# A Fourier mixing layer and a routed MLP on one core: earlier half-batch routing, another order of the first loads, and wider pieces of w2

## The chip, the cores and the metric

The kernel runs on one core of a Trainium2 chip. The metric is the device time of one execution in microseconds. The profile comes from one further execution, whose own span is longer.

## The reference

The input x has shape 8 x 2496 x 256. The first half is the real part of a two-dimensional Fourier transform of each batch. The 19,968 resulting rows go through eight experts, one for each row. All arithmetic is f32.

```python
X = np.fft.fft(np.fft.fft(x, axis=1), axis=2).real.reshape(B * S, D)   # S = 2496, D = 256
logits = X @ w_gate                        # 8 experts
e = argmax(logits, axis=1)
gate = softmax(logits)[row, e[row]]
y[row] = gate[row] * (relu(X[row] @ w1[e[row]]) @ w2[e[row]])   # w1: 256 x 1024, w2: 1024 x 256
```

## The kernel before, in words

Each batch passes three stages, and the rows of all batches then pass in blocks through the experts.

`first(b)` loads x in three quarters `q`. For each quarter `load_x` issues `xl`, a plain load on SP's queue, and `xh`, an indirect gather on POOL's queue that brings the mirrored rows; quarter 0 also loads `x0`. `fold` and `fold_d` add and subtract on VectorE (L290 to L284), `half1` multiplies by the table `w1` of waves (matmuls `s`), ScalarE copies the result to `t1` (L307), and `t1` is written to a DRAM scratch `Td` (L337). Each step ends in a `yield`; there are 12 steps, three for each of four values of `q`.

`regroup(b, h)` reads `Td` back in another layout into `t4` (L350); it needs all three writes. `second(b)` starts with `turn_last` (matmul `pr`), then makes ten windows of 128 rows in two halves of five (matmuls `p`, results `zz`, `rows` and the logits `lg`). After each half `route` takes the arg max, ranks the rows within each expert by matmuls `rk`, and scatters the rows into the DRAM buffer `Xs` by ten indirect stores on POOL's queue (L454). Every expert has its own region of `Xs`. `base` holds how far each region is filled.

`plan` turns `base` on VectorE into a table of blocks: first row and expert of each. `rounds()` fixes how many blocks of which size are made after which batch. Before: two of 256 rows and four of 128 after batch 0, four of 256 after batch 1, then blocks of 512, and 256s and 128s to end with; 66 blocks in all.

`experts` goes through the blocks in that order. For each block `fetch` reads row and expert from the table on SP (L509, L510) and issues three loads on SP's queue: the rows `xb` (L512), `w1` (L515) and `w2` (L517), 1 MB each for the weights, with three buffers of each. `turn` transposes the rows on TensorE; matmuls `ph` and a relu, by turns on ScalarE (L572) and VectorE (L570), give `hT`; matmuls `py` give the output, which ScalarE scales and POOL scatters. In the profile an f32 matmul of the code appears as two matmul instructions.

The order on each engine is the order in which the program issues instructions: `tc.manual_schedule()` leaves it as written. The loop at the end takes one step of `experts` at a time (a `yield 1` or `2` counts as work, `yield 0` as none) and then runs some steps of `side`, which holds the next batch's `first`, this batch's `second` and the plans. `sent` and `taken` tell the framework which scatters a fetch of rows must wait for: those up to its own round's.

At the start, before the change, seven steps of `first(1)` run ahead of `second(0)`, the rest beside it:

```python
    early = ahead_of(1)
    for _ in range(7):
        next(early)
    for k, _ in enumerate(second(0)):
        if k % 2 == 0:
            next(early, None)
```

Of the kernel before, what the change touches and what calls it, by code (L numbers as in the profile page):

```python
# [130 lines left out]
def rounds():  # L131

    want = [((256, 2), (128, 4)), ((256, 4),)] + [((512, B),)] * (B - 2)
    plan, used = [], 0

    def full(done, size):
        return max(0, -(-(done - used - E * (size - 1)) // size))

    for b in range(B):
        done = (b + 1) * S
        now = []
        for size, most in want[b]:
            k = min(full(done, size), most)
            if k:
                now.append((size, k, False))
            used += size * k
        if b == B - 1:
            k = full(done, BLK)  # L150
            used += BLK * k
            now.append((BLK, k, False))
            now.append((REST, (NT - used + E * (REST - 1)) // REST, True))
        plan.append(now)
    return plan


def in_order():

    todo = []  # L160
    for b, now in enumerate(rounds()):
        parts = [[(b, size, last, i) for i in range(k)] for size, k, last in now]
        if b == B - 1:
            few, many = parts[-2:]
            n = len(many) // len(few)
            rest = [x for i, y in enumerate(few) for x in [y] + many[n * i:n * (i + 1)]] + many[n * len(few):]
            parts = parts[:-2] + [rest]
        todo += sum(parts, [])
    return todo


TICKS = 44
WARM = 12
MOST = max(k for now in rounds() for _, k, _ in now)


# [15 lines left out]
def kernel(ctx: ExitStack, tc, x, w_gate, w1, w2, out):  # L192
# [18 lines left out]
    def put_row(dst, idx, rows, last, group):  # L211
        return unordered(pool.indirect_dma_start(  # L212
            out=dst, out_offset=bass.IndirectOffsetOnAxis(ap=idx, axis=0),
            in_=rows, in_offset=None, bounds_check=last, oob_is_err=False), group)


    def sent(ins, b):
        tc.declare_no_dep(ins, group="taken", reason="no block before this batch's round has these rows")
        tc.add_to_no_dep_group(f"xs{b}", ins)

    def taken(ins, b):
        ins = getattr(ins, "ins", ins)
        if b + 1 < B:
            tc.declare_no_dep(ins, group=f"xs{b + 1}", reason="a block has rows of its round's batches alone")
        tc.add_to_no_dep_group("taken", ins)


# [83 lines left out]
    def load(b, q):  # L311
        if b < B:
            ahead[b, q] = load_x(b, q)
        if b < B and q == 0:
            n = NP if b + 1 < B else NA
            x0 = xp.tile([NP, D], F32, tag="x0", name="x0")
            nc.sync.dma_start(out=x0[0:n], in_=xall[NA * b:NA * b + n, 0])
            ahead[b, "x0"] = x0[0:NA]

    def first(b):  # L320

        pm0 = xp.tile([NA, D], F32, tag="pm0", name="pm0")
        for q in range(NQ + 1):
            f = iter(())
            if q < NQ:
                xl, xh = ahead.pop((b, q))
                f = fold(xl, xh, q)
            next(f, None)
            yield
            if q:  # L330
                t1 = xp.tile([NP, 4, D], F32, tag="t1", name="t1")
                half1(b, q - 1, 0, pm, pm0, t1)
            next(f, None)
            yield
            if q:
                half1(b, q - 1, 1, pm, pm0, t1)
                nc.sync.dma_start(out=Td[b][:, 4 * (q - 1) * D:4 * q * D], in_=t1[:].rearrange("p j d -> p (j d)"))  # L337
                load(b + 1, q - 1)
            next(f, None)
            if q == 1:  # L340
                fold_d(pm0[:], ahead.pop((b, "x0")), 1)
            pm = xh
            yield
# [68 lines left out]
    def route(b, h, rows, lg):  # L412
# [38 lines left out]
        vec.tensor_tensor(nxt[:], rk[:, NSL], base[:], op=ALU.add)  # L451
        base = nxt
        for s in range(NSL):
            sent(put_row(Xs, pi[:, s:s + 1], rows[:, s], E * CAP - 1, "xs"), b)  # L454
            yield


# [47 lines left out]
        tabs[b, size, last] = tab  # L505

    def fetch(b, size, tab, i):
        n = size // 128
        row = nc.sync.value_load(tab[:, 0, i:i + 1], min_val=0, max_val=ROWS - size)  # L509
        ev = nc.sync.value_load(tab[:, 1, i:i + 1], min_val=0, max_val=E - 1)  # L510
        xb = bp.tile([128, BIG // 128, W], F32, tag="xb", name="xb", bufs=3)
        taken(nc.sync.dma_start(out=xb[:, 0:n].rearrange("p t c -> p (t c)"),  # L512
                                in_=Xs[ds(row, size)].rearrange("(p t) c -> p (t c)", t=n)), b)
        w1_sb = bp.tile([128, 2, F], F32, tag="w1", name="w1_sb", bufs=3)
        nc.sync.dma_start(out=w1_sb[:], in_=w1[ds(ev, 1)].rearrange("o (c p) f -> p (o c) f", p=128))  # L515
        w2_sb = bp.tile([128, FC, D], F32, tag="w2", name="w2_sb", bufs=3)
        nc.sync.dma_start(out=w2_sb[:], in_=w2[ds(ev, 1)].rearrange("o (c p) d -> p (o c) d", p=128))  # L517
        return xb, w1_sb, w2_sb

    def turn(size, xb):  # L520

# [11 lines left out]
    def experts(todo):  # L533
# [2 lines left out]

        got, xT = [], None

        def fetch_some(k, most=3):

            while k + len(got) < len(todo) and len(got) < most and todo[k + len(got)][:3] in tabs:
                b, size, last, at = todo[k + len(got)]
                got.append(fetch(b, size, tabs[b, size, last], at))

        for k, (b, size, last, at) in enumerate(todo):
            n, m = size // 128, BIG // size
            if not k:
                while todo[0][:3] not in tabs:
                    yield 0
                fetch_some(0)  # L550
                for _ in range(9):
                    yield 0
                for xT in turn(size, got[0][0]):
                    pass
# [7 lines left out]
            for f in range(FC // m):  # L562
                ph = psh.tile([128, m, size], F32, tag="h", name="ph")
                for j in range(m):
                    for c in range(2):
                        mm(ph[:, j], w1_sb[:, c, (m * f + j) * 128:(m * f + j + 1) * 128], xT[:, c, 0:size],
                           c == 0, c == 1)
                o = hT[:, m * f:m * (f + 1), 0:size]
                if f % 2:
                    vec.tensor_scalar(o, ph[:], 0.0, None, op0=ALU.max)  # L570
                else:
                    act.activation(o, ph[:], ACTF.Relu)  # L572
                yield 1
# [17 lines left out]
    def pads(b):  # L591

        ti = cp.tile([128, E], I32, name="ti")
        vec.tensor_scalar(ti[:], base[:], con["lane"][:], None, op0=ALU.add)
        for e in range(E):
            sent(put_row(Xs, ti[:, e:e + 1], pad[:], ROWS - 1, "xs"), b)
            yield

    def woven(*parts):
# [7 lines left out]

    def close(b):

        for size, k, last in rounds()[b]:  # L610
            yield from plan(b, size, k, last)

    def ahead_of(b):

# [16 lines left out]
    vec.memset(ones[:], 1.0)  # L631
    act.dma_start(out=con["w1"][:, 0:4], in_=waves[:, 0:4])
    load(0, 0)
    act.dma_start(out=con["w1"][:, 4:], in_=waves[:, 4:])
    for _ in range(WARM):
        pw = psy.tile([128, D], F32, tag="y", name="py")
        mm(pw[:], ones[:], bc(ones[:], 1, 2))
    load(0, 1)
    load(0, 2)
    act.dma_start(out=con["rt"][:], in_=const_dram("rt", consts["rt"]))  # L640
    act.dma_start(out=wg[:], in_=w_gate.rearrange("(c p) e -> p c e", p=128))
    nc.sync.dma_start(out=table[:], in_=const_dram("table", packed))
    nc.sync.dma_start(out=bt[:], in_=const_dram("blocks", cv))
    sent(unordered(nc.sync.dma_start(
        out=Xs[E * CAP:].rearrange("(k p) w -> p k w", k=BLK // 128), in_=bc(pad[:], 1, BLK // 128)), "xs"), 0)
    warm = cp.tile([1, 1], F32, name="warm")
    vec.memset(warm[:], 0.0)
    act.activation(warm[:], warm[:], ACTF.Exp)
# [2 lines left out]
    todo = in_order()  # L651
    for _ in first(0):
        pass
    regroup(0, 0)
    regroup(0, 1)
    vec.tensor_copy(tri[:], con["tri"][:])
    for c in range(2):
        pg = pm_.tile([128, E], F32, tag="m", name="pg")
# [5 lines left out]
            vec.tensor_scalar(con["rd"][:, c, to + E:to + 2 * E], pg[:], con["sgn"][:], None, op0=ALU.mult)  # L664
        else:
            vec.tensor_copy(con["rd"][:, c, to + E:to + 2 * E], pg[:])
    early = ahead_of(1)
    for _ in range(7):
        next(early)
    for k, _ in enumerate(second(0)):  # L670
        if k % 2 == 0:
            next(early, None)
    work = experts(todo)
    for b in range(1, B):

        side, done, due = mixed(b), 0, 0.0
        if b == 1:
            side = woven(close(0), chain(early, side))
        total = 16 * sum(k * size for size, k, _ in rounds()[b - 1]) / BIG
        while done < total:  # L680
            w = next(work)
            done += w
            due += TICKS * w / (0.7 * total) if w else 1
            while due >= 1:
                next(side, None)
                due -= 1
        for _ in side:
            pass
# [27 lines left out]
```

## Time and profile before

| | before |
|---|---|
| time, median of 3 runs | 1382.49 us (1381.39 to 1383.51) |
| span of the profiled execution | 1422.8 us |
| TensorE busy | 1338.3 us (94%), clock 0.970 in the mean |
| VectorE, ScalarE, GpSimd busy | 382.6, 283.8, 350.8 us |
| moved by DMA | 248.81 MB in 134,517 packets, 93,839 of them under 2 KB |

TensorE (PE) is nearly always busy, but matmuls are pipelined, so the share alone does not say how fast it works. The granted clock has to be read beside it: it is low in some slices of the first 230 us and full in the rest. SP and its queue carry plain loads and stores, ACT's queue a few loads at the start, POOL's queue every gather and scatter.

### The profile page before, as it was taken

Reading aid. Unit: us, or ns where it says so; the run is one execution under the profiler, and the core shown is the slowest. Engines: PE = TensorE matmul, PEld = TensorE weight load, DVE = VectorE, ACT = ScalarE, POOL = GpSimd, SP = SyncE. Lnnn points to the kernel's source line nnn. Section 1 sums busy time; section 2 is a strip of 40 time slices with the busy share of each in tenths; the row PEclk is TensorE's granted clock in tenths of the full one; section 3 lists DMA queues with packets and bytes.
Section 4 is the critical chain, followed back from the end, with each engine's and each line's share of the span. In section 5 each row is a group of like instructions: output and inputs, shape, how many; then the busy total and the mean of one; then the engine's idle time right before and its main releaser. Section 6 shows DMA issues by size and latency. Waiting matters only on the chain.

```text
span 1422.8 us, 17245 instructions
## 1 busy us (share of the span) xinstructions
PE 1338.3 (94%) x6186; PEld 1016.2 (71%) x6186; DVE 382.6 (27%) x1206; ACT 283.8 (20%) x656; POOL 350.8 (25%) x360
## 2 busy tenths in 40 slices
PE   4658798998999999999999999999999999999998
PEld 3557687776676667776676667776667779999997
DVE  3453243333242222322132321333211111111111
ACT  1322122132132211221122211221111111111111
POOL 1243314333314311234113311224221111111111
PEclk9768899999999999999999999999999999999999
DMA  8859777644546452561435342333442248788883
GB/s 228 204 184 291 242 240 235 246 135 117 209 131 206 135 173 90 179 187 64 168 105 166 131 175 89 108 111 107 168 143 93 89 136 269 264 265 267 268 272 102
DMA packets 134517, 248.81 MB, mean 175 GB/s; under 512 B 11245, under 2 KB 93839, under 8 KB 134432
## 3 DMA queue, kind: packets, MB, share of 16 engines
q1 hardware_dynamic: 114438, 194.38, 42.8%
q0 software_dynamic: 19344, 52.37, 10.8%
q10 hardware_dynamic: 650, 0.97, 0.3%
q8 instruction: 49, 0.80, 0.2%
q14 instruction: 36, 0.29, 0.1%
HBM read 194.28 MB, written 54.83 MB: 175 GB/s over the span
## 4 chain that ended last, share of the span: by engine, by line
PE 55%; issue 31%; POOL 5%; another core or an unknown queue 3%; DMA 2%; DVE 2%; ACT 1%; POOLq 0%; SPq 0%; DVEq 0%; ACTq 0%
PE py L197 22%; PE ph L197 22%; PE p L197 6%; POOL out_dram L212 4%; PE s L197 3%; PE pt L528 1%; DMA xh<-in_x_dram,ix 1%; POOL Xs L212 1%; DMA Td<-t 1%; DMA t<-Td 0%; DVE hT L570 0%; DVE rows L406 0%; DMA xb<-Xs 0%; POOLq L212 0%
## 5 line engine op out<-in xcount | busy, mean ns | idle before, releaser
L197 PE MATMUL ph<-xT,w_sb 128*128 128x512 f32 (+2 forms) x2112 | 589.3, 433 | 7.7 <-ACT hT L572 2.3
L197 PE MATMUL py<-w_sb,hT 128*128 128x256 f32 x2608 | 584.6, 381 | 8.5 <-DVE hT L570 8.5
L197 PEld LDWEIGHTS py<-w_sb,hT 128*128 128x128 f32 x2608 | 489.4, 191 | 72.1 <-DVE hT L570 9.3
L197 PEld LDWEIGHTS ph<-xT,w_sb 128*128 128x128 f32 x2112 | 340.2, 192 | 205.3 <-issue 176.5
L212 POOL DMA_INDIRECT out_dram<-y,ro x163 | 159.2, 977 | 861.7 <-ACT y L585 832.5
L570 DVE TENSOR_SCALAR hT<-ph 128x512 f32<-128x512 f32 x163 | 112.7, 692 | 716.6 <-issue 350.5
L585 ACT ACTIVATE y<-py,xb 128x256 f32<-128x256 f32 x163 | 77.3, 474 | 625.0 <-PE py L197 537.5
L212 POOL DMA_INDIRECT Xs<-rows,pi x160 | 159.1, 994 | 122.8 <-issue 76.1
L572 ACT ACTIVATE hT<-ph 128x512 f32<-128x512 f32 x163 | 97.3, 597 | 324.1 <-PE ph L197 287.7
L529 DVE TENSOR_SCALAR xT<-pt,table 128x512 f32<-128x512 f32 (+1 forms) x94 | 63.3, 674 | 66.7 <-PE pt L528 63.8
L197 PE MATMUL s<-xh,w 104*112 104x256 f32 (+2 forms) x208 | 62.0, 424 | 17.6 <-DVE xh L284 13.9
L197 PEld LDWEIGHTS p<-table,t 120*128 120x128 f32 x352 | 56.8, 211 | 29.2 <-issue 19.8
L197 PE MATMUL p<-table,zz 128*128 128x145 f32 (+1 forms) x320 | 60.0, 315 | 15.7 <-issue 8.0
L197 PE MATMUL p<-table,t 120*128 120x120 f32 (+1 forms) x352 | 59.6, 296 | 11.1 <-issue 4.1
L404 DVE COPY lg<-p 128x16 f32<-128x16 f32 x80 | 14.0, 175 | 203.8 <-ACT zs L401 148.0
L197 PEld LDWEIGHTS p<-table,zz 128*128 128x128 f32 x320 | 48.7, 207 | 20.0 <-issue 11.1
L197 PEld LDWEIGHTS s<-xh,w 104*112 104x112 f32 x208 | 39.8, 205 | 30.3 <-DVE xh L284 15.1
L528 PEld LDWEIGHTS pt<-table,xb 128*128 128x128 f32 x326 | 40.7, 142 | 17.7 <-issue 11.6
L528 PE MATMUL pt<-table,xb 128*128 128x128 f32 x326 | 51.6, 274 | 1.7 <-DMA xb<-Xs 1.7
L406 DVE SCALAR_TENSOR_TENSOR rows<-p,zs 128x129 f32<-128x129 f32 x160 | 48.4, 344 | 1.6 <-issue 0.6
L274 POOL DMA_INDIRECT xh<-in_x_dram,ix x24 | 24.3, 1014 | 80.4 <-PE s L197 59.8
L375 ACT COPY zz<-p 128x240 f32<-128x240 f32 (+1 forms) x88 | 31.1, 353 | 54.1 <-PE p L197 36.8
(84 smaller groups left out, 333.1 us busy)
## 6 DMA issues: line engine op xcount, KB each, us to landing
w_sb<-in_moe_w_dram SPq DMA_DIRECT2D x132, 1024.0 KB
xb<-Xs SPq DMA_DIRECT2D x28, 516.0 KB
Td<-t SPq DMA_DIRECT2D x24, 448.0 KB
xl<-in_x_dram SPq DMA_DIRECT2D x21, 448.0 KB
t<-Td SPq DMA_DIRECT2D x8, 720.0 KB
t<-Td SPq DMA_DIRECT2D x8, 600.0 KB
xb<-Xs SPq DMA_DIRECT2D x13, 258.0 KB
xb<-Xs SPq DMA_DIRECT2D x25, 129.0 KB
```

Source lines behind the costliest of these rows:

```text
L197: nc.tensor.matmul(o, lhsT=lhsT, rhs=rhs, start=start, stop=stop, **kw)
L212: return unordered(pool.indirect_dma_start(out=dst, out_offset=bass.IndirectOffsetOnAxis(ap=idx, axis=0), in_=rows, in_offset=None, bounds ...
L274: pool.indirect_dma_start(out=xh[:].rearrange("p j d -> p (j d)"), out_offset=None, in_=xrows, in_offset=bass.IndirectOffsetOnAxis(ap=ix[: ...
L375: act.copy(zz[:, :, g * GP:g * GP + n], p2[:])
L404: vec.tensor_copy(lg[:, k:k + 2], p3[:, NY:NY + 2 * E].rearrange("p (m e) -> p m e", m=2))
L406: vec.scalar_tensor_tensor(rows[:, k + m, 0:NY], p3[:, 0:NY], zs[:, 0:1], zs[:, 1:], op0=ALU.add, op1=op)
L528: nc.tensor.transpose(pt[:, c, t], xb[:, 2 * h + t, c * 128:(c + 1) * 128], ident[:])
L529: vec.tensor_scalar(xT[:, :, 256 * h:256 * h + 128 * n], pt[:].rearrange("p c t k -> p c (t k)"), con["alt"][:], None, op0=ALU.mult)
L570: vec.tensor_scalar(o, ph[:], 0.0, None, op0=ALU.max)
L572: act.activation(o, ph[:], ACTF.Relu)
L585: act.activation(y[:, i], py[:], ACTF.Copy, scale=xb[:, i, D + 1:D + 2])
```

## The change

- Blocks: after the first half of batch 0 a round of two 128-row blocks is planned and started; one 256-row block fewer follows, 67 blocks in all. Rounds are numbered from this one, so batch `b` closes round `b + 1`; `sent` and `taken` are shifted to match.
- Start: `x0` is loaded with quarter 1 and folded one quarter later. Only the first piece of the wave table stays on ACT's queue; its rest, `table`, `rt` and `wg` go to SP's queue between and behind the x of batch 0. The loads of batch 1 are no longer issued inside `first(0)`: quarters 0 and 1 come ahead of the two reads of `Td[0]` on SP, quarter 2 behind them, then the block constants and the padding rows of `Xs`. The warming matmuls go from 12 to 16.
- `Td` of batches 0 and 1 is written from ACT's queue.
- `first(1)` runs wholly inside `second(0)`, at the steps listed in `FILL`. From step 11 on the plan of the new round runs beside the first half's scatters; after step 20 the fetches of its blocks are issued, then the reads of `Td[1]`.
- `fetch` is split: for the very first block the weights are requested ahead of the rows, for others rows first as before.
- A partition of `w2` takes two neighbouring rows, so that a piece is 2 KB instead of 1 KB; to match, the stationary operand of `ph` takes every second column of `w1`.

```diff
-    want = [((256, 2), (128, 4)), ((256, 4),)] + [((512, B),)] * (B - 2)
+    want = [((128, 2),), ((256, 1), (128, 4)), ((256, 4),)] + [((512, B),)] * (B - 2)
...
-    for b in range(B):
-        done = (b + 1) * S
+    for b in range(B + 1):
+        done = b * S if b else 2 * 128 * HW - NB
...
-WARM = 12
+WARM = 16
+FILL = (0, 1, 2, 3, 4, 5, 6, 8, 9, 10, 11, 12, 13)
+
+AFTER = 5 + HW
...
-        if b + 1 < B:
-            tc.declare_no_dep(ins, group=f"xs{b + 1}", reason="a block has rows of its round's batches alone")
+        for later in range(b + 1, min(b + 3, B + 1)):
+            tc.declare_no_dep(ins, group=f"xs{later}", reason="a block has rows of its round's batches alone")
...
-        if b < B and q == 0:
+        if b < B and q == 1:
...
-                nc.sync.dma_start(out=Td[b][:, 4 * (q - 1) * D:4 * q * D], in_=t1[:].rearrange("p j d -> p (j d)"))
-                load(b + 1, q - 1)
+                (nc.sync if b > 1 else act).dma_start(out=Td[b][:, 4 * (q - 1) * D:4 * q * D], in_=t1[:].rearrange("p j d -> p (j d)"))
+                if b:
+                    load(b + 1, q - 1)
             next(f, None)
-            if q == 1:
+            if q == 2:
...
-            sent(put_row(Xs, pi[:, s:s + 1], rows[:, s], E * CAP - 1, "xs"), b)
+            sent(put_row(Xs, pi[:, s:s + 1], rows[:, s], E * CAP - 1, "xs"), b + 1 if b or h else 0)
...
-        nc.sync.dma_start(out=w2_sb[:], in_=w2[ds(ev, 1)].rearrange("o (c p) d -> p (o c) d", p=128))
-        return xb, w1_sb, w2_sb
+        return xb
+
+    def chunk(w1_sb, c, f):
+        return w1_sb[:, c, f // 2 * 256 + f % 2:(f // 2 + 1) * 256:2]
...
+        nc.sync.dma_start(out=w2_sb[:].rearrange("p (c j) d -> p c (j d)", j=2),
+                          in_=w2[ds(ev, 1)].rearrange("o (c p j) d -> p (o c) (j d)", p=128, j=2))
...
-                fetch_some(0)
-                for _ in range(9):
+                fetch_some(0, first=True)
+                for _ in range(5):
...
-                        mm(ph[:, j], w1_sb[:, c, (m * f + j) * 128:(m * f + j + 1) * 128], xT[:, c, 0:size],
-                           c == 0, c == 1)
+                        mm(ph[:, j], chunk(w1_sb, c, m * f + j), xT[:, c, 0:size], c == 0, c == 1)
...
     load(0, 0)
-    act.dma_start(out=con["w1"][:, 4:], in_=waves[:, 4:])
+    load(0, 1)
+    nc.sync.dma_start(out=con["w1"][:, 4:], in_=waves[:, 4:])
+    load(0, 2)
+    nc.sync.dma_start(out=table[:], in_=const_dram("table", packed))
+    nc.sync.dma_start(out=con["rt"][:], in_=const_dram("rt", consts["rt"]))
+    nc.sync.dma_start(out=wg[:], in_=w_gate.rearrange("(c p) e -> p c e", p=128))
...
+    load(1, 0)
+    load(1, 1)
     regroup(0, 0)
     regroup(0, 1)
+    load(1, 2)
+    nc.sync.dma_start(out=bt[:], in_=const_dram("blocks", cv))
...
-    early = ahead_of(1)
-    for _ in range(7):
-        next(early)
+    early = first(1)
+    work = experts(todo)
+    first_blocks = plan(0, *rounds()[0][0])
     for k, _ in enumerate(second(0)):
-        if k % 2 == 0:
+        if k in FILL:
             next(early, None)
-    work = experts(todo)
+        if k > AFTER:
+            next(first_blocks, None)
+        if k == AFTER + 2 * HW:
+            for _ in early:
+                pass
+            next(work)
+            regroup(1, 0)
+            regroup(1, 1)
```

## The prediction

> **What bounds the kernel now.** I read the page's slices first, then the busy times by stage, then the timeline of the first 112 us and the sync queue's own waits. The stages, with columns stretch, length, busy us (and count) of PE, PEld, DVE, ACT, POOL, then TensorE clock, DMA share and GB/s:
>
> ```profile
> 0.00:17.60 17.60, 2.74 (x12) 1.23 (x12) 3.03 (x9) 1.49 (x2) 3.54 (x8) 1.00 0.92 215
> 17.60:29.50 11.90, 11.20 (x35) 8.10 (x35) 5.74 (x17) 3.52 (x6) 2.35 (x3) 1.00 0.76 202
> 29.50:44.70 15.20, 4.33 (x12) 2.82 (x12) 8.38 (x20) 1.17 (x2) 1.67 (x2) 0.55 0.90 238
> 44.70:70.00 25.30, 20.49 (x132) 17.88 (x132) 11.91 (x59) 12.76 (x39) 7.06 (x8) 0.84 0.81 205
> 70.00:100.80 30.80, 15.43 (x57) 13.02 (x57) 17.59 (x73) 5.47 (x17) 17.86 (x16) 0.58 0.50 169
> 100.80:250.00 149.20, 129.38 (x727) 114.58 (x728) 50.02 (x189) 34.86 (x91) 48.35 (x49) 0.91 0.81 253
> 250.00:1416.00 1166.00, 1153.62 (x5210) 857.87 (x5209) 285.96 (x842) 224.02 (x499) 269.02 (x276) 1.00 0.49 164
> ```
>
> From 250 us to the last output TensorE is busy 1153.6 of 1166 us at full clock: its backlog sets the end, and only what it loses earlier can be recovered. Before 250 us it is idle for 66.4 us (250 less the six busy sums, 183.6), of which 46.6 fall before 100.8 us, when the first expert matmul runs. The timeline tells what it waits for (start, length, engine, line, operation):
>
> ```profile
> 14.99 1.22 DVE L290 TENSOR_TENSOR xl<-xl,xh 104x1020 f32<-104x1020 f32 x1 [13.69 <-DMA xh<-in_x_dram,ix]
> 29.46 0.31 SPq L337 DMA_DIRECT2D Td<-t  x1
> 38.04 0.91 SPq L350 DMA_DIRECT2D t<-Td  x2
> 44.74 0.54 PE L197 MATMUL pr<-t,table 120*120 120x6 f32 x2 [7.31 <-DMA t<-Td]
> 93.50 0.39 SPq L512 DMA_DIRECT2D xb<-Xs  x1
> 94.08 0.41 SPq L515 DMA_DIRECT2D w_sb<-in_moe_w_dram  x1
> 100.79 0.48 PE L197 MATMUL ph<-xT,w_sb 128*128 128x256 f32 x1 [1.11 <-DVE xT L529]
> 111.31 3.62 PE L197 MATMUL py<-w_sb,hT 128*128 128x256 f32 x16
> ```
>
> The serial start is visible: x at 15, the last Td write takes 29.5 to 38.0, its read back to 44.7, and then no weight is requested before 94.1. The sync queue's waits name the reason: it stood in front of the first plan and of the row scatter, with the weights queued behind.
>
> ```profile
> SPq L509 <- DVE p_n L500: 17.0, 1, 17.0
> SPq L512 <- DMA Xs<-rows,pi: 8.1, 1, 8.1
> ```
>
> [...]
>
> **The change part by part.**
>
> *Start.* ACT's queue keeps only 182 KB of w1; the rest of w1 (500 KB), rt, wg and table stand on SP behind the x that is used first, x0 behind the second quarter, pad rows and bt far later. The first xh (416 KB) landed at 15.0 while three queues shared 215 GB/s. With two in competition I put it 2 to 3 us sooner (bounds 0 to 5; a loss is excluded, since less stands beside it). Four warming matmuls add 1 us inside the idle 13.6. Fold and matmuls of batch 0 follow at their pace (29.5-17.7): last t1 at about 26.5.
>
> *Td and batch 1.* Td of batches 0 and 1 goes out from ACT; SP issues loads (1,0) and (1,1), then the two reads of Td, then (1,2). The last Td write took 8.6 us beside them. What must move by its landing: 4.2 MB of start, 1.4 MB of Td and 2.3 MB of batch 1 (two xl, three xh, x0), 7.9 MB; at 238 GB/s 33 us (bounds 31, by Td's own 8.6 less its share of neighbours, and 38, no change). The first read back (720 KB) took 6.6 with 600 KB and batch 1 beside it; I take 4, so `pr` at 37 instead of 44.7. Load (1,2), bt and the pad rows (258 KB) follow on SP, where nothing else waits until 60. Each issue costs ACT some 0.3 us, six in all, beside PE waits: nothing.
>
> *First half.* Before ran 7 steps of first(1) ahead; now all 12 lie inside second(0), so DVE folds of 2.7 us a quarter come between windows: five windows at 0.8 us DVE plus 3.9 us of folds, after 4 us from `pr` to the first window (44.7 to 52.4 less 3.8 us of s matmuls): 41 to 49. Route and the remaining folds: 3.5 + 2.4 + waits, 55. The steps of first(1) also issue the x of batch 2 now, on SP (1.5 MB, before any weights) and POOL (three gathers of 1.0 us, the last between two scatters); the DMA stage they fall in is the one before had them in. Before's first half ended at 62.5 (L451 base).
>
> *A plan more.* Its DVE work ran from 76.1 to 82.7 with a fold of 2.9 in it: 3.7 by itself, I take 4.5. It ends near 60; the value loads follow and the first w1 leaves at 61.5 instead of 94.1. The second half's windows and route stand behind the plan on DVE: they end at 69 instead of 76. That DVE delay costs PE nothing: it has no other work until rows arrive.
>
> *Blocks.* Ten scatters at 1.28 us start-to-start (63.42 to 75.01), with one xh gather between: 55.6 to 70. A block of the first round waits for this half's scatter alone: its rows can be fetched at 72, its weights lie there already, transposes at 76, `ph` at 76.5 to 80 (32 matmuls in 3.73 us). On SP, xb of block 1, its 2 MB of weights, then both reads of Td(1) are queued behind that scatter: issue 74.5; 2 MB at 350 GB/s take 6, so Td(1)'s first half is there at 82.5. In before it was issued at 63.2. PE reaches `pr` of batch 1 after block 0's `ph` (five side steps ahead of the block, two per `ph` group) and waits from 80 to 82.5; `py` and block 1 are queued behind.
>
> *Sum.* At 82.5 us PE has done one block's `ph` and transposes, 3.8 us. Before, at 100.8, had done, of the following batches, 28 `p` of 120 columns and 4 transposes at 0.11 us each, 16 `p` of 145 columns at 0.125 and 8 `s` at 0.216: 7.2 us (the pace from the chain of waits: `pt` x4 in 0.44, `py` x16, 256 columns, in 3.46). The change is at that point 3.4 us later, at 85.9: 14.9 us ahead. One block more (67 for 66) costs PE about 0.3 us, and 2.1 MB, 8 us of transfer at 253 GB/s, hidden because the first 4 MB of weights move from 94 to 110 us into 61 to 80, a stretch at 169 to 205 GB/s. The stage 100.8 to 250 loses 20 us idle and 11.6 of clock (0.09 of 129); I keep these as they are: net **14.5 us**. Made against the profiled span 1422.8, which is 40 us above the runs at 1382.5; I carry the difference over in microseconds, 1382.5 - 14.5 = **1368**.
>
> *2 KB pieces of w2.* A stretch of 4 KB pieces alone moved 350 GB/s, one of 1 KB pieces (407 of 498 packets) 386: no gain is shown. Bounds: 1.05 MB at the one rate or the other differ by 0.3 us, on some ten blocks that wait for transfers 3 us, in either direction; I take 0.
>
> *Stationary step of two.* LDWEIGHTS of a 128-column `ph` comes every 0.117 us (32 in 3.76), as often as its matmul. [...] I take nothing.
>
> **Rivals.**
>
> *The step of two slows the load.* [...] For it: PEld is busy 3.76 of 3.73 us there. [...] Chance 0.10.
>
> *The moved wait eats the gain.* Td(1)'s read now stands behind the scatter, two xb and 2 MB on SP; if instruction flow or scatter slip by 15 us, PE stands at `pr` as long as it did before. In the trace DVE stood 16.5 us at 146 with the releaser unknown, so slips of this size exist. Also the case that the two blocks don't run early because all of second(0) is ahead of them. 1376 to 1392, around 1382; chance 0.16: 0.07 within 0.2% and 0.09 above.
>
> *The late losses go too.* With weights ahead of rows and transfers begun 30 us sooner, half of the 31 us lost from 100.8 to 250 vanishes: 1368 - 16 = 1352. Against: per 128-row block 2.1 MB for 7.3 us of PE, 290 GB/s, beside the FFT's transfers. Chance 0.16.
>
> **How the numbers follow.** Forecast 0.58 (1358 to 1378 by itself), rivals 0.10, 0.16, 0.16. A measurement of this kernel can tell 0.2%, 2.8 us. Faster: 0.58 + 0.16 = 0.74; same 0.07; slower 0.09 + 0.10 = 0.19. The range from 1346 to 1390 leaves out the stride case and the tails of the others.
>
> **What would show it.** Right: first `pr` near 37 us, first w1 issue near 61 (not 94), first `ph` near 76, `pr` of batch 1 near 82 with a DMA t<-Td wait of 2 to 3 us; packets under 2 KB falling by 66 x 1024 to some 26,000; 128-column `ph` still 32 in 3.7 us. Wrong: LDWEIGHTS of `ph` above 3.8 us for 32, `pr` of batch 1 past 95, or TensorE idle before 250 us still above 60.

## The result and the profile after

The change took 1395.49 us (median of four runs, 1390.69 to 1396.66) against 1383.00 for the kernel before on the same chip (1381.39 to 1385.85). The ratio is 1.0081, with an interval from 1.0052 to 1.0111. It is slower by 0.8%, or 12.5 us; a gain of 14.5 us had been forecast.

Chips differ here, and without that several numbers below can't be understood. On some chips the kernel before takes 1383 to 1384 us, and its profile has no wait whose releaser is unknown (the profile writes "remote"). On others it takes 1410 to 1425 us, and its profiles there have 48 to 89 us of such waits, summed over the engines. I call them quiet and noisy chips; among the experiments only one chip was met at two times, and it was noisy both times, so it could also be a matter of the hour. By these marks the comparison above was on a quiet chip, and the profile of before that I predicted from, with its span of 1422.8 us, came from a noisy one.

The stages of the profile after, in the same stretches and columns as shown of before:

```profile
0.00:17.60 17.60, 4.68 (x19) 2.50 (x20) 3.05 (x9) 1.49 (x2) 3.53 (x8) 0.74 0.90 218
17.60:29.50 11.90, 10.14 (x37) 7.30 (x35) 6.75 (x19) 3.51 (x6) 2.92 (x3) 0.67 0.94 265
29.50:44.70 15.20, 5.66 (x30) 5.42 (x31) 3.23 (x9) 2.44 (x8) 0.00 (x0) 0.66 0.91 229
44.70:70.00 25.30, 16.03 (x112) 13.31 (x110) 20.53 (x97) 11.08 (x33) 11.81 (x12) 0.86 0.78 239
70.00:100.80 30.80, 14.26 (x71) 13.10 (x71) 10.81 (x42) 1.60 (x4) 13.35 (x12) 0.67 0.89 262
100.80:250.00 149.20, 137.94 (x825) 123.99 (x824) 62.51 (x238) 41.34 (x108) 58.67 (x59) 0.98 0.77 254
```

The last stage looks like a large gain: 137.94 us busy for 129.38. It is none of the change's doing, as the experiments show: on a quiet chip the kernel before is busier there still (144.57 us, in e11). The stage from 70 to 100.8, where the first block was to come early, is no better filled than before (14.26 for 15.43), although DMA now moves 262 GB/s there instead of 169. The timeline tells why (start, length, engine, line, operation, and in brackets the idle time ahead):

```profile
39.04 0.54 PE L201 MATMUL pr<-t,table 120*120 120x6 f32 x2 [10.51 <-DMA t<-Td]
61.67 0.41 SPq L516 DMA_DIRECT2D w_sb<-in_moe_w_dram  x1
75.33 1.51 SPq L526 DMA_DIRECT2D xb<-Xs  x2
77.76 0.69 PE L541 MATMUL pt<-table,xb 128*128 128x128 f32 x2 [9.87 <-DMA xb<-Xs]
78.78 7.16 SPq L355 DMA_DIRECT2D t<-Td  x2
79.03 6.05 PE L201 MATMUL ph<-xT,w_sb 128*128 128x128 f32 x32 [0.57 <-DVE ro L581]
96.96 0.57 PE L201 MATMUL pr<-t,table 120*120 120x6 f32 x2 [8.21 <-DMA t<-Td]
```

The start, the first weights and the first expert matmul came nearly when forecast. But TensorE stands twice: 9.87 us for the first rows, which came 16 us after the request for the weights, and 8.21 us at `pr` of batch 1, whose t was read only behind the rows. In the waits of TensorE over the whole span these are the two largest rows:

```profile
PE pt L541 <- DMA xb<-Xs: 19.4, 5, 9.9
PE pr L201 <- DMA t<-Td: 18.7, 2, 10.5
```

### The profile page after: what moved, and what is told of

It reads as the page before. It is cut to its first block, busy times and chain, and to the rows that moved or that the text cites. A ratio compares the mean times of both kernels' runs of the same rounds, so it can differ in the third digit from the quotient of the medians.

```text
span 1394.0 us, 17358 instructions
## 1 busy us (share of the span) xinstructions
PE 1326.5 (95%) x6222; PEld 1020.1 (73%) x6222; DVE 385.9 (28%) x1228; ACT 283.4 (20%) x656; POOL 349.9 (25%) x360
## 2 busy tenths in 40 slices
DMA packets 101671, 250.92 MB, mean 180 GB/s; under 512 B 11293, under 2 KB 26559, under 8 KB 101584
## 4 chain that ended last, share of the span: by engine, by line
PE 52%; issue 31%; POOL 7%; DMA 6%; DVE 2%; POOLq 0%; ACT 0%; SPq 0%; ACTq 0%; DVEq 0%
PE py L201 21%; PE ph L201 21%; PE p L201 5%; POOL out_dram L216 5%; PE s L201 3%; POOL Xs L216 2%; DMA t<-Td 2%; PE pt L541 1%; DMA xb<-Xs 1%; DMA xh<-in_x_dram,ix 1%; DMA Xs<-rows,pi 1%; DMA w_sb<-in_moe_w_dram 0%; POOLq L216 0%; DMA Td<-t 0%; PE rk L201 0%
## 5 line engine op out<-in xcount | busy, mean ns | idle before, releaser
L201 PE MATMUL ph<-xT,w_sb 128*128 128x128 f32 (+2 forms) x2144 | 592.4, 431 | 1.0 <-DVE ro L581 0.6
L201 PEld LDWEIGHTS ph<-xT,w_sb 128*128 128x128 f32 x2144 | 356.4, 198 | 187.4 <-issue 172.5
L201 PE MATMUL s<-xh,w 104*112 104x256 f32 (+2 forms) x208 | 56.3, 392 | 13.3 <-DVE xh L288 12.0
L201 PEld LDWEIGHTS p<-table,t 120*128 120x128 f32 x352 | 52.7, 198 | 15.5 <-issue 11.8
L201 PE MATMUL p<-table,zz 128*128 128x145 f32 (+1 forms) x320 | 55.8, 299 | 2.6 <-DVE rows L411 2.1
L201 PE MATMUL p<-table,t 120*128 120x120 f32 (+1 forms) x352 | 55.3, 282 | 0.3 <-ACT t L373 0.3
L201 PEld LDWEIGHTS s<-xh,w 104*112 104x112 f32 x208 | 36.4, 188 | 25.5 <-DVE xh L288 13.3
L201 PEld LDWEIGHTS p<-table,zz 128*128 128x128 f32 x320 | 45.4, 194 | 6.1 <-issue 2.4
L311 ACT COPY t<-s 112x512 f32<-112x512 f32 x48 | 28.0, 583 | 49.2 <-PE s L201 48.0
```

What stands on the lines that cost most here:

```text
L201: nc.tensor.matmul(o, lhsT=lhsT, rhs=rhs, start=start, stop=stop, **kw)
L311: act.copy(t1[:, 2 * half:2 * half + 2], ps[:])
```

## Experiments

Eighteen runs. "Losses" below are TensorE's idle time plus its busy time times (1 - granted clock), summed over six stretches up to 350 us, with the mean clock of each; behind that the backlog runs without gaps on quiet chips, down to the last outputs. Ratios are to the kernel before on the same chip.

**The kernel before, again (four profiles).** No edit. The question was whether the 31 us that before lost between 100.8 and 250 us belong to the kernel.

> The kernel before once more, unchanged, for a second profile. Theory A, that the first profile (1422.8 us beside runs of 1383) held waits that ordinary runs do not have: span 1380 to 1388 us, the 16.5 us wait of VectorE at 146 us and the other waits without a known releaser gone, TensorE idle before 250 us some 40 us less than the 66.4 us of the first profile. Rival, that profiling itself costs 40 us: span again near 1420.

> The kernel before, unchanged, for a profile on this chip. Theory D: waits without a known releaser in the first 350 us if the runs here are at 1420 us, and none if they are at 1383 us.

> The kernel before, unchanged, for a profile on another chip. Theory D: at 1383 us without waits of unknown releaser, or at 1420 us with some 30 us of them on the path in the first 350 us.

> The kernel before for a profile. Theory D: if runs are near 1383 us, no waits of unknown releaser, TensorE idle before 250 us about 35 us less than the 66.4 us of the first profile, and the first expert matmul still at 95 to 101 us. Rival: these waits are there at 1383 us too, and the difference is the rate of the transfers.

The first three fell on noisy chips (1415.26, 1424.98 and 1420.28 us) and show waits like these, which are those of the first profile of before, in the view of all waits (us in total, times, longest):

```profile
DVE hT L570 <- remote: 41.2, 5, 16.5
ACT zz L375 <- remote: 16.9, 4, 5.8
ACT y L585 <- remote: 13.3, 2, 8.2
```

So e1 alone could not tell theory A from its rival. The fourth fell on a quiet chip: 1386.25 us beside timed runs of 1383.94, so profiling does not cost 40 us; no remote wait, and these stages:

```profile
70.00:100.00 30.00, 13.01 (x56) 10.89 (x56) 17.08 (x73) 5.44 (x17) 18.72 (x16) 0.63 0.50 156
100.00:150.00 50.00, 47.44 (x268) 42.54 (x269) 20.07 (x83) 13.05 (x33) 21.56 (x22) 0.92 1.02 326
150.00:250.00 100.00, 97.14 (x567) 86.82 (x566) 39.80 (x137) 25.03 (x63) 37.60 (x38) 1.00 0.81 265
```

From 100 to 250 us before loses 5.4 us idle and 3.8 of clock (0.08 of 47.44), not 31. The rest went with the remote waits. One expectation missed: TensorE's idle time before 250 us is 55.8 us, 11 less than in the first profile and not 35; another 11 us are losses of clock, and 9 lie between 250 and 350 us.

The kept traces tell one thing about the remote waits. In the first profile of before and in e1, e8 and e9, every one of them (18, 14, 14 and 9) ends at an update of one semaphore that TensorE alone updates, up to 9.3 us behind the end that the profile gives TensorE's last instruction ahead of it. So these engines waited for TensorE, and its signal came later than its profile says. Why, and why on some chips only, stays unknown.

**The change in parts, first on noisy chips.** Batch 1's read ahead of the rows; the change without 2 KB pieces and step of two; these two alone on the kernel before; the change itself; the start alone (new order of loads, Td on ACT, no early blocks, 1 KB pieces).

```
e2:  -            next(work)
                  regroup(1, 0)
                  regroup(1, 1)
     +            next(work)
e3:  w2 loaded by "o (c p) d -> p (o c) d", chunk = w1_sb[:, c, f * 128:(f + 1) * 128]
e4:  before, with the change's w2 load and chunk()
e6:  before, with WARM = 16, the change's loads (bt and the pad rows behind load(1, 2)), and in first():
     +  (nc.sync if b > 1 else act).dma_start(out=Td[b]..., in_=t1...)
e7:  e2 and e3 together
```

> The change, with both reads of Td of batch 1 issued on the sync queue ahead of the first blocks' weights and rows. Theory B, that the change loses its gain because this read stands behind 2 MB of weights and a row scatter: the first matmul of batch 1's second stage at about 75 to 80 us instead of 97, and 6 to 12 us less than the change, 1384 to 1389 us. Rival, that the first weights then come later by the 1.3 MB read and the stretch is bound by transfers: within 3 us of the change.

> The change with the old 1 KB pieces of w2 and the old contiguous columns of w1. Theory C, that the step of two costs 0.18 us in each 128-row block (3.58 us before, 3.76 after, for 32 matmuls) and wide pieces gain nothing: 27 x 0.18 = 5 us less than the change, about 1390 us. Rival, that wide pieces speed up the early weights: 2 to 5 us more than the change.

> The kernel before with the 2 KB pieces of w2 and the step of two alone. Theory C: 25 x 0.18 = 4.5 us more than before, about 1387 us. Rival, that wide pieces help where weights are waited for: 1 to 4 us less than before.

> The change itself, unchanged, beside the kernel before on one chip. Theory D, that two kinds of chip or of session exist, one in which waits without a known releaser hold all engines for some 30 us in the first 350 us and one without them, and that the change gains only in the first kind: ratio to before 0.990 to 0.996 where before takes about 1420 us (such waits in the trace), 1.006 to 1.011 where before takes about 1383 us (no such waits). Rival, that the ratio is the same everywhere and the first comparison was an accident: about 0.992 in both.

> The kernel before with the new order of the first loads, Td of batches 0 and 1 from ACT and x of batch 1 behind it, and nothing else: no early blocks, seven steps of batch 1 still ahead, 1 KB pieces. Theory B (the loss lies in the early blocks, the gain in the start): 4 to 7 us less than before, the first matmul of batch 0's second stage at about 39 us. Rival, that the start gains nothing because the second stage waits for x of batch 1 instead, which seven steps ahead of it need: within 2 us of before.

> The change with 1 KB pieces and contiguous columns, and with both reads of Td of batch 1 ahead of the first blocks' weights and rows. Theory B and C together: 5 us for the columns and 2 to 6 for the read, 7 to 11 us less than the change. Rival, that only the columns matter: 5 us less than the change.

| run | ratio | interval |
|---|---|---|
| read ahead of rows (e2) | 0.9922 | 0.9892 to 0.9951 |
| change, 1 KB pieces (e3) | 0.9921 | 0.9893 to 0.9949 |
| before, 2 KB pieces and step of two (e4) | 1.0031 | 1.0018 to 1.0044 |
| change (e5) | 0.9960 | 0.9944 to 0.9975 |
| start alone (e6) | 0.9970 | 0.9953 to 0.9986 |
| read ahead, 1 KB pieces (e7) | 0.9910 | 0.9878 to 0.9942 |

The change itself is faster here by 0.4%, on a quiet chip slower by 0.8%. Theory D had foretold both before e5 ran (0.990 to 0.996, and 1.006 to 1.011), after e2 and e3 had come out below the kernel before; it means that a comparison of parts is worth something only within one sort of chip. The pieces with the step of two cost 3.6 us (1423.24 for 1419.63); taken out of the change they give that or some more back (0.9921 for 0.9960, on two chips). e7 had been expected 7 to 11 us below the change and came 5.0 below it on the same chip (1407.55 for 1412.58), the figure of its rival, by which only the columns matter. As e2, e3 and e7 lie within each other's intervals, the moved read and the pieces don't add up on noisy chips.

**The same parts on a quiet chip.** The kernels of e5, e6 and e3 once more.

> The change. Theory D: near 1395 us if before is near 1383 us, 0.994 to 0.998 of before if before is above 1405 us.

> The new start alone. Theory B (the loss lies in the early blocks): 3 to 6 us less than before on either kind of chip. Rival, that the start loses where before has no waits: 2 to 10 us more than before at 1383 us.

> The change with 1 KB pieces and contiguous columns. Theory C: 4 to 6 us less than the change on either kind of chip. Rival: no more than 2 us less where there are no such waits.

| | median us | ratio (interval) | losses to 100 | 100 to 150 | 150 to 250 | 250 to 350 |
|---|---|---|---|---|---|---|
| before (e11) | 1383.94 | 1 | 60.3, some 4 too low (see "The granted clock") | 6.4 | 2.9 | 0.6 |
| change (e12) | 1395.34 | 1.0072 (1.0047 to 1.0097) | 62.3 | 1.7 | 9.7 | 0.4 |
| start alone (e13) | 1379.33 | 0.9975 (0.9964 to 0.9987) | 59.4 | 0.0 | 2.6 | 0.4 |
| change, 1 KB (e14) | 1391.59 | 1.0044 (1.0012 to 1.0076) | 61.6 | 2.2 | 12.9 | 1.1 |

The first column takes the row of before from its runs, its losses from the profile of e11. So the 11.4 us are: start alone -4.6, early blocks with their new order +12.3 (e14 less e13), pieces and step of two +3.7 (e12 less e14; the intervals of these two overlap, so this part is clear only in e4). Between e13 and e14 the losses rise by 15.4 us and the spans by 15.4 (1375.7 to 1391.1); 10.3 of it lies between 150 and 250 us, far behind the early blocks.

What TensorE does ahead of its first block in the start alone (timeline of TensorE):

```profile
62.75 0.54 PE L197 MATMUL pr<-t,table 120*120 120x6 f32 x2
63.15 2.90 PE L197 MATMUL p<-table,t 120*128 120x120 f32 x12
...
76.39 2.05 PE L197 MATMUL s<-xh,w 104*112 104x256 f32 x4
79.00 1.21 PE L197 MATMUL p<-table,t 120*128 120x120 f32 x4 [0.57 <-DVE rows L407]
80.01 0.41 PE L197 MATMUL pr<-t,table 120*120 120x5 f32 x2
80.28 1.32 PE L197 MATMUL p<-table,zz 128*128 128x145 f32 x4
90.73 1.11 PE L529 MATMUL pt<-table,xb 128*128 128x128 f32 x4 [9.13 <-DMA xb<-Xs]
```

and in the change, on the same chip:

```profile
77.40 0.69 PE L541 MATMUL pt<-table,xb 128*128 128x128 f32 x2 [9.89 <-DMA xb<-Xs]
78.67 6.27 PE L201 MATMUL ph<-xT,w_sb 128*128 128x128 f32 x32 [0.58 <-DVE ro L581]
84.78 0.38 PE L541 MATMUL pt<-table,xb 128*128 128x128 f32 x2
85.00 3.62 PE L201 MATMUL py<-w_sb,hT 128*128 128x256 f32 x16
95.62 0.57 PE L201 MATMUL pr<-t,table 120*120 120x6 f32 x2 [7.00 <-DMA t<-Td]
```

Both wait 9 to 10 us for rows. But the start alone has `pr` and four of the ten windows of batch 1's second step behind it by then, in time in which the change is idle or works on a block. The change starts its first block 13.3 us sooner and `pr` of batch 1 32.9 us later (95.62 for 62.75). All that hangs on batch 1 follows: batch 2's Td is read back at 144.3 instead of 120.3, and from 100 to 150 us DMA moves 232 GB/s where the start alone moves 333:

```profile
100.00:150.00 50.00, 48.77 (x322) 44.58 (x320) 23.39 (x94) 17.83 (x48) 19.20 (x20) 0.99 0.73 232
150.00:250.00 100.00, 93.08 (x515) 83.03 (x516) 40.14 (x145) 23.52 (x60) 39.47 (x40) 0.97 0.80 268
```

(the change), and

```profile
100.00:150.00 50.00, 50.00 (x307) 45.19 (x306) 22.57 (x94) 13.11 (x33) 26.43 (x27) 1.00 1.02 333
150.00:250.00 100.00, 97.41 (x537) 83.41 (x535) 39.49 (x131) 25.71 (x64) 34.09 (x34) 1.00 0.80 265
```

(the start alone). The sync queue of the change stands meanwhile, from 100 to 260 us, ahead of the writes of Td (L341), until ScalarE has copied `pr` into t, and ahead of the plans:

```profile
SPq L341 <- ACT t L373: 34.9, 2, 19.1
...
SPq L524 <- DVE p_n L505: 26.1, 2, 13.9
```

In the start alone the same two waits are 16.0 and 11.0 us, and its longest one (25.8 us) is for ScalarE's `y`, that is, for a buffer of rows to come free: there the queue is ahead of the work. Rows that are requested late are waited for: in that stretch TensorE's waits for xb are 6.6 us in the change, 9.1 in e14 and 1.3 in the start alone.

**First weights ahead of the first rows.** The start alone, its first block's weights issued ahead of its rows.

```
-                got.append(fetch(b, size, tabs[b, size, last], at))
+                x = (b, size, tabs[b, size, last], at)
+                if k + len(got):
+                    got.append((fetch_rows(*x), *fetch(*x)))
+                else:
+                    w = fetch(*x)
+                    got.append((fetch_rows(*x), *w))
```

> The kernel before with the new start (as in the run of the start alone) and, besides, the very first block's weights ahead of its rows; no early blocks, 1 KB pieces. Theory E, that the early blocks are not needed, since what they gain is that weights are requested before the scatter ends: first w1 leaves 10 us sooner than with the start alone (at about 80 instead of 91 us), first expert matmul unchanged at about 97 us because rows still come after the scatter, 2 to 5 us less than the start alone, thus 0.990 to 0.996 of before where before takes 1420 us. Rival, that TensorE then waits for rows instead: within 2 us of the start alone.

> The new start with the first block's weights ahead of its rows, no early blocks, 1 KB pieces. On the last chip it was at 0.9976 of before where the start alone is at 0.997. Theory E: 2 to 4 us less than the start alone, 1375 to 1377 us where before takes 1384, since the 2.4 us wait of the first expert matmul for weights goes. Rival, that it waits for rows and the later weights instead: 1378 to 1381 us.

Noisy chip: 0.9976 (0.9959 to 0.9993); quiet chip: 0.9964 (0.9947 to 0.9981), 1378.76 us. The weights leave at 74.33 instead of 86.49, and `pt` still waits 8.97 us for xb (9.13 without). The 2.42 us for which `ph` waited for weights in e13 are gone, without a gain. Rows set the first block, and this edit gives nothing that could be measured beside the start alone.

**The order of steps (F), and the read moved.** The change with 1 KB pieces and the seven steps of first(1) ahead, as the kernel before had them; then batch 1's read ahead of the rows as well.

```
+FILL = (0, 2, 4, 6, 8, 10)
...
+    for _ in range(7):
+        next(early)
e16 also:  next(work) behind regroup(1, 0) and regroup(1, 1)
```

> The change with 1 KB pieces and contiguous columns, and with seven steps of batch 1's first stage ahead of batch 0's second stage again, the rest in every second step; early blocks kept. Theory F, that the order of these steps makes half of the 12 us: TensorE idle before 45 us falls by some 5 us, and the time is 4 to 7 us less than the change with 1 KB pieces (1385 to 1388 us where before takes 1384, 0.987 to 0.989 of before where it takes 1410 to 1420). Rival, that these steps are done in time anyway and the early blocks make all of it: within 2 us of the change with 1 KB pieces, 1390 to 1393 us (0.992).

> The same, and both reads of Td of batch 1 ahead of the first blocks' weights and rows. Theory B: 2 to 5 us less than the run before it, since the matmul pr of batch 1 no longer waits for them behind 2 MB. Rival, that rows and weights then come as much later: within 2 us of it.

e15: 1392.15 us, 1.0057 (1.0033 to 1.0081), as e14 within the intervals. Theory F, that the folds of first(1) inside second(0) cost the time, fell. e16: 1386.72 us, 1.0020 (1.0007 to 1.0032): the read ahead of the rows gives 5.4 us back. Its first `pr`:

```profile
81.01 0.69 PE L540 MATMUL pt<-table,xb 128*128 128x128 f32 x2 [11.10 <-DMA xb<-Xs]
...
91.79 0.28 PE L201 MATMUL pr<-t,table 120*120 120x6 f32 x2
```

No wait stands before `pr` any more, but it runs only at 91.79, because the block stands ahead of it in TensorE's order.

**17 side steps ahead of the first block.** e16 with that order changed.

```
-                for _ in range(5):
+                for _ in range(17):
```

> The change with 1 KB pieces, seven steps of first(1) ahead and the read of batch 1's Td ahead of the first rows, as in e16, and in addition 17 side steps instead of 5 ahead of the first block. In e16 TensorE stood 11.1 us before the transposes of block 0 (rows until 81.0) while batch 1's t had been read from 58.8 on; its `pr` stood behind the block in TensorE's queue and ran at 91.8. Theory G: the early blocks lose because the first block stands in front of batch 1's second step, which in the kernel before and in the start alone fills this idle time (first `pr` of batch 1 at 72 and 63 us there, 97 in the change), and so batch 2's steps, its plan and the rows of later blocks come late. It expects `pr` of batch 1 before 75 us, the wait for xb shortened to 4 to 8 us, TensorE's losses to 350 us (idle and clock) at 63 to 68 instead of 73.5, and a ratio to before of 0.994 to 0.999. Rival H: the losses come from the transfers themselves (rows and weights of the early blocks beside Td and the scatters), whatever TensorE's order is; it expects the ratio at 1.001 to 1.004 again and the read at the same price.

This run fell on a noisy chip: 1401.5 us for 1410.45, 0.9942 (0.9919 to 0.9965). The local part came as G says:

```profile
72.53 0.55 PE L201 MATMUL pr<-t,table 120*120 120x6 f32 x2
...
82.58 0.63 PE L540 MATMUL pt<-table,xb 128*128 128x128 f32 x2
89.84 3.78 PE L201 MATMUL ph<-xT,w_sb 128*128 128x128 f32 x16 [6.64 <-DVE ro L580]
```

`pr` runs at 72.53 and the wait for xb is gone, but 6.64 us of waiting for DVE stand in its place ahead of `ph`: the 17 steps stand ahead of the block in VectorE's order too, and it works on folds, plan and rows until 89.33, when it comes to xT of the block. The losses to 350 us are 82.9, far above the 63 to 68 that G expected; on this sort of chip the change itself has 82.4 (e5). The ratio lies in the range of G, 0.994 to 0.999, but on the same chip so does that of the change (0.9960), and e7, without this edit, is lower still (0.9910). So the run doesn't decide between G and H, and the same kernel on a quiet chip wasn't tried.

## Why the prediction was wrong

All three signs of being wrong that I had named came: `pr` of batch 1 at 96.96 (past 95), 3.95 us of LDWEIGHTS for 32 (above 3.8), and 61.3 us of idle TensorE before 250 us (above 60; before has 55.8 on a quiet chip).

**Start, and the first half.** Right. The first `pr` ran at 39.04 (forecast 37), the first weights left at 61.67 (61.5), and the start alone gives 4.6 us (ratio 0.9975). The last write of Td of batch 0, now on ACT's queue, took 4.3 us from 27.9 on, where it had taken 8.6 on SP's; so the reads left at 32.3 us, for 38.0 in before (I had put 33, an estimate from bytes; no run of before has a Td write on ACT's queue); t then took 6.7 us as before, where I had put 4. The x came 1.2 us sooner (first matmul `s` at 16.52 for 17.67), less than the 2 to 3 of the forecast.

**The granted clock.** Read wrongly in the first two stages of before. The view gives 1.00 there, with TensorE's longest gap, 13.6 us, in the first of them, and I took it as it stood. But the trace has no record of the clock before 27.7 us (26.4 in e11), and the pace says that it was low: in e11 22 matmuls `s` from 17.54 us on take 9.60 us, in the start alone 22 from 15.92 take 9.62, and there the clock is on record, 0.56 from 17.6 to 26 us. At 49.91 us in the change, where the trace has the full clock, 8 of them take 1.98. At 0.56 the 8.9 us from 17.54 to 26.4 are some 4 us that the losses of before leave out.

**Blocks.** Wrong, and with it most of the loss. The first `ph` at 79.03 is near the forecast 76.5. But `pr` of batch 1 ran at 96.96, where I had put 82.5 and named "past 95" as the sign of being wrong. I had counted 2 MB at 350 GB/s ahead of the read, 6 us from 74.5, and t there 2 us later. In e12 the reads left at 78.47. What DMA moved beside them from 77 to 91.5 us (KB each, median us from issue to landing):

```profile
DMA packets 2168, 4.03 MB, mean 278 GB/s; under 512 B 193, under 2 KB 1179, under 8 KB 2167
...
w_sb<-in_moe_w_dram SPq DMA_DIRECT2D x2, 1024.0 KB, 9.8
t<-Td SPq DMA_DIRECT2D x1, 720.0 KB
t<-Td SPq DMA_DIRECT2D x1, 600.0 KB
xb<-Xs SPq DMA_DIRECT2D x1, 258.0 KB, 8.0
Xs<-rows,pi POOLq DMA_INDIRECT x7, 7.6
```

That is twice my bytes at four fifths of my rate, 14.5 us, and t was there at 95.62, 17 us after its issue: both halves of t, the rows and the second half's scatters were in it, which I had left out. The rival of the moved wait has this wait, with a slip of 15 us; it got 0.16. It laid the slip to instruction flow or scatter, though, not to the bytes in front of the read, and its range, 1376 to 1392, ends below the time measured. e16 against e15 prices the moved read at 5.4 us.

**The sum at 100.8 us.** Wrong. I set one block's 3.8 us of `ph` against 7.2 us of batch 1's work that would be missing, and took 14.9 us as the lead. On one quiet chip the losses to 100 us are 62.3 us in the change and 60.3 in before, or some 64 with the clock put right, so neither kernel is ahead by more than some 2 us there (the change's four more warming matmuls, 0.9 us of its busy time, do none of the work). The early block wasn't put into idle time: it took the place of batch 1's second step, which in before (`pr` at 72.06 and 86.79 in e11) and in the start alone fills the wait for the first rows. I had listed that step's matmuls as work to be made up, but not what hangs on them: batch 2's Td (read at 144.3 us, for 127.7 in before), the next plan, and the rows of the blocks after 150 us. There the change loses 6.8 us more than before (9.7 for 2.9). Of the 12.3 us of the early blocks, 5.4 are the moved read by e16. For the remaining 7 to 8 us (e16 stands 8.0 behind the start with weights first on the same chip) the late second step of batch 1 fits the timelines of e12 to e16, but the run that should have shown it (e18) didn't decide. Rival H, the transfers themselves, stays open.

**The 31 us between 100.8 and 250.** Wrong, and the base of the sum with it. I kept this loss as equal in both kernels. On a quiet chip before loses some 9 us there, and the change 11. The profile was 40 us above the runs; I saw this and carried the difference over in microseconds, where a second look would have shown that the waits with no known releaser didn't belong to the timed runs beside it. That the early blocks gain some 7 us over the start alone on noisy chips (0.9921 for 0.9970, on two of them; on one and the same chip, with the read ahead of the rows, 0.9910 for 0.9970) and lose 12 on a quiet one is measured; why isn't known. That they fill time which remote waits leave idle is only argued.

**2 KB pieces.** Right: 26,559 packets under 2 KB, forecast some 26,000, and no gain showed.

**Stationary step of two.** The rival was right that the step slows the load: 3.95 us for 32 LDWEIGHTS, where before has 3.76. Groups of `ph` with 128 columns in the change with the step (e12), and then without (e14):

```profile
L201 PE MATMUL ph<-xT,w_sb 128*128 128x128 f32 x864 | 110.3, 288 | 0.6 <-DVE ro L581 0.6
```

```profile
L201 PE MATMUL ph<-xT,w_sb 128*128 128x128 f32 x864 | 105.0, 281 | 0.6 <-DVE ro L580 0.6
```

5.3 us in 27 blocks, or 0.006 us for each of the 864 loads. I took 0, a term that no run shows. Within a block it is seen in the distance from the first `ph` to the `pt` that follows, 3.76 us in the change and 3.58 in before:

```profile
1292.75 3.95 PEld L201 LDWEIGHTS ph<-xT,w_sb 128*128 128x128 f32 x32
1292.96 3.92 PE L201 MATMUL ph<-xT,w_sb 128*128 128x128 f32 x32
1296.72 0.38 PE L541 MATMUL pt<-table,xb 128*128 128x128 f32 x2
```

```profile
1323.48 3.73 PE L197 MATMUL ph<-xT,w_sb 128*128 128x128 f32 x32
1327.06 0.38 PE L528 MATMUL pt<-table,xb 128*128 128x128 f32 x2
```

Groups of 256 columns are unchanged (380 and 379 ns), those of 512 too (594 and 593). The cost of pieces and step together (3.7 us quiet, 3.6 noisy, where the interval of e4 excludes 0) is a little less than this; nothing is left for the pieces to cost. For a 128-column stationary operand in f32 this case measures some 5% (110.3 us for 105.0). My sum had no slack on TensorE, so even this small term went through to the end.

## What to carry to other kernels

When work is pulled forward on an engine that runs in order, list what used to fill that time and what hangs on it two stages on; as far as these runs tell, the price is paid where those rows run out, here 60 to 150 us later. When a transfer is moved behind others, count all bytes that move beside it, in every queue, not only the ones that the edit names: here 4.03 MB in 14.5 us, where I had counted 2 MB. If the profile's span lies 3% above the timed runs, take a second profile before making a sum, and don't carry its waits with an unknown releaser over to runs that may not have them. Where a view gives a full clock behind a long gap (here 1.00 behind 13.6 us, at a pace that goes with 0.56 on record in another run), hold it against the pace of equal matmuls elsewhere. Of the kernels tried on quiet chips the start alone (1379.33 us, 0.9975) and the start with weights first (1378.76, 0.9964) beat both the kernel before and the change; these two can't be told apart.

## What the runs showed that was not expected

The same kernel, before, takes 1384 or 1410 to 1425 us by the chip or the hour, and the sign of a comparison turns with it: the change is 1.0072 on one chip and 0.9960 on another. The issue of the two reads of Td took SP 7.16 us directly behind two loads of 1 MB, where the same two took 0.91 at 38 us in the kernel before. Part of that can be a wait: a semaphore on which the second read waits was updated 4.2 us after its start. In the start alone a Td write behind four such loads took SP 5.23 us, and the trace shows no wait that ended in it; so there the issue held the queue's engine, and all that stood behind it, by itself. What it waits for isn't shown.
